# Turning q and k on TensorE instead of by DMA, with three score products over half the partitions

## The chip, the cores and the metric

The kernel runs on one core of a Trainium2 chip. The metric is the device time of one launch in microseconds (us). The engines are named as in the profile: PE is TensorE's matmuls and PEld its weight loads, DVE is VectorE, ACT ScalarE, POOL GpSimd, SP SyncE, which issues every DMA of this kernel from one queue.

## What is computed

Attention with queries that are averaged in pairs, over 4 batches, 8 heads, 1152 keys and a head size of 64, and then two feed-forward layers over the 2304 tokens that come out of it (width 512, inner width 2048). All in float32:

```python
q_pool = q.reshape(B, H, S // 2, 2, D).mean(axis=3)
scores = scale * np.matmul(q_pool, k.transpose(0, 1, 3, 2))
attn = np.exp(scores - np.max(scores, axis=-1, keepdims=True))
attn = attn / (np.sum(attn, axis=-1, keepdims=True) + 1e-09)
x = np.matmul(attn, v)            # heads side by side: 2304 x 512
h = x @ w_in1;  x = (h * np.cos(h)) @ w_out1
h = x @ w_in2;  out = (h / (1.0 + np.exp(-h))) @ w_out2
```

## The kernel before

TensorE gets float16 only. Every float32 operand is scaled by a power of two and split in a high part, rounded to float16, and a low part, the rest in float16; a product of two such operands is taken from three or four products of parts, summed in PSUM.

**Pairs of heads.** The attention goes through 16 pairs, head j and head j + 4 of one batch. `pair_loads` (L317) loads q, k and v of a pair from SP's queue. `pair_prep` (L341) adds neighbouring rows of q on POOL, takes absolute maxima on DVE, makes the common scales of the pair with a small float32 matmul (`mean_scales`, L122, tile `bm`), and then splits. For q, ACT writes the high part twice and DVE the low part, with a copy, into `qn` (L376 to L383), so that a row of 128 values holds high and low part of one head side by side, and a second arrangement low and high. One DMA transpose (L385) turns its 18 blocks of 128 x 128 into `qT`. For k, `kn` is made the same way and a second DMA transpose (L395) of 18 blocks makes `kT`. v needs no turning (`do_v`, L369).

**Tiles.** A pair has nine score tiles: four of 128 queries for each head, and one that holds the last 64 queries of both. `tile_scores` (L406) multiplies over all 128 partitions: qT's first arrangement (high over low) against kT (high over low) gives two products at once, the second arrangement (low over high) the other two. That is two passes over 1152 keys in pieces of 512, 512 and 128 columns, six matmuls. The remainder tile does it for each head on 64 columns of the array, twelve matmuls. The scores stand in `sp`, a PSUM tile with one buffer. DVE reads it (`sc`, L431), ACT takes the exponential (L438) and the high part (L444), POOL the low part (`hl`, L449), a DMA transpose of 18 blocks turns both (`hlT`, L451), and TensorE multiplies by v (`pv`, L462 and L466) four tiles later.

**Around it.** In the first four pairs DVE, ACT and POOL also decode the weights of the first layer. From the second batch on, `share` puts two units of the first layer between two tiles: `g1_unit` (L534) is 12 matmuls into `h`, `g2_unit1` (L594) 12 into `y`. Tiles `h`, `bm` and the other small matmuls share the two buffers of the PSUM pool `ps_h`. What is left of the first layer then runs beside the decoding of the second layer's weights, and the second layer follows. While pair n is worked on, `prep_then_load(n + 1)` prepares the next pair and then loads the one after it.

The order on each engine is made by the tile framework's scheduler when the kernel is built, from priorities (`P_SC`, `P_EX` and so on) and its own estimates; every engine, and SP's queue, then runs its list strictly in that order.

## Time and profile before

| | us |
|---|---|
| median of 3 runs | 1474.19 (1473.89 to 1474.35) |
| the profiled execution | 1469.55 |
| its span, first to last instruction | 1467.3 |

| engine | busy us | share of the span |
|---|---|---|
| PE | 1187.7 | 81% |
| DVE | 990.1 | 67% |
| ACT | 788.3 | 54% |
| POOL | 584.3 | 40% |
| DMA, queue of SP | | 59.5% of 16 engines |

The span has two halves of different kind. In the page's 40 slices the DMA engines are busy for 7 to 9 tenths or more up to slice 24, that is until about 900 us: this is the attention, with the first layer between its tiles. From slice 30 on PE is at 9 tenths or more and the others at 1 to 3: this is the second layer. A share of busy time over the whole span mixes the two, so it is read by stretch.

### The profile page before, as it was taken

The numbers are of one execution on the slowest core, as the hardware profiler recorded it, in microseconds if no ns is written. First come the engines' busy times: TensorE is split into PE (matmuls) and PEld (weight loads), VectorE is DVE, ScalarE is ACT, GpSimd is POOL, SyncE is SP. The second block draws the span as 40 slices with busy tenths as digits, with TensorE's granted clock in tenths as the row PEclk, the third lists the DMA queues.
The fourth block names the chain that finished last, engine by engine and source line by source line (L and its number), as shares of the span: only waits on it lengthen the run. The fifth ranks groups of instructions, "written<-read, shape, count | busy, mean of one in ns | idle before, by whom it ended". The sixth has DMA issues, their size and how long they took to land. (4 is left out here: it accounts for less than half of the span.)

```text
span 1467.3 us, 25115 instructions
## 1 busy us (share of the span) xinstructions
PE 1187.7 (81%) x10070; PEld 867.4 (59%) x10070; DVE 990.1 (67%) x1822; ACT 788.3 (54%) x1005; POOL 584.3 (40%) x329
## 2 busy tenths in 40 slices
PE   1555554787987697788988886788899999999998
PEld 0333332475765465566666765676776666666665
DVE  7999998687775778777888874788963233332312
ACT  3766767568775687767687773645541111111110
POOL 1765664545655466556456452464530000000000
PEclk9875656799998799999999997999999999999999
DMA  8898996978899899869979875324310000000001
GB/s 251 176 229 171 213 233 117 188 146 153 161 179 182 161 189 211 164 127 176 192 146 197 183 133 94 115 87 130 101 46 15 28 29 30 29 30 15 15 1 29
DMA packets 493589, 186.19 MB, mean 127 GB/s; under 512 B 433568, under 2 KB 468384, under 8 KB 493472
## 3 DMA queue, kind: packets, MB, share of 16 engines
q1 hardware_dynamic: 493472, 184.59, 59.5%
q8 instruction: 79, 1.29, 0.4%
q14 instruction: 38, 0.31, 0.1%
HBM read 66.58 MB, written 9.44 MB: 52 GB/s over the span
## 5 line engine op out<-in xcount | busy, mean ns | idle before, releaser
L449 POOL TENSOR_TENSOR hl<-sc,hl 128x1152 f16<-128x1152 f32 x144 | 369.5, 2572 | 250.4 <-ACT hl L444 166.3
L542 PEld LDWEIGHTS <-ih 128*128 128x128 f16 x2304 | 229.9, 101 | 80.3 <-issue 19.3
L555 ACT ACTIVATE hk<-h,ca 128x512 f32<-128x512 f32 x144 | 97.9, 681 | 303.8 <-PE h L542 303.4
L416 PE MATMUL sp<-kT,qT 128*128 128x512 f16 (+1 forms) x768 | 182.2, 383 | 94.6 <-DVE sc L431 83.4
L431 DVE TENSOR_SCALAR_CACHE_REDUCE sc<-sp,psu 128x1152 f32<-128x1152 f32 x144 | 202.9, 1409 | 70.1 <-PE sp L416 55.9
L462 PE MATMUL pv<-vt,hlT 128*128 128x130 f16 (+1 forms) x1440 | 187.3, 243 | 73.5 <-DMA hlT<-hl 61.3
L438 ACT ACTIVATE sc<-sc,nb 128x1152 f32<-128x1152 f32 x144 | 179.8, 1250 | 118.8 <-DVE nb L435 80.7
L462 PEld LDWEIGHTS <-hlT 128*128 128x128 f16 (+1 forms) x1440 | 149.9, 114 | 104.3 <-DMA hlT<-hl 80.1
L542 PE MATMUL h<-xT,ih 128*128 128x256 f16 x1024 | 196.5, 289 | 11.1 <-ACT hk L555 7.1
L542 PE MATMUL h<-ys,ih 128*128 128x256 f16 x1152 | 198.0, 273 | 0.8 <-ACT hk L555 0.8
L466 PE MATMUL pv<-vt,hlT 128*128 128x65 f16 (+1 forms) x1440 | 180.0, 212 | 0.0
L416 PEld LDWEIGHTS <-qT 128*128 128x128 f16 x768 | 76.6, 111 | 168.5 <-issue 131.0
L444 ACT ACTIVATE hl<-sc 128x1152 f16<-128x1152 f32 x144 | 165.3, 1154 | 8.2 <-DMA xT<-xn 3.5
L602 PE MATMUL y<-gh,oh 128*128 128x256 f16 x576 | 159.7, 277 | 6.3 <-ACT y L611 6.3
L602 PE MATMUL y<-gl,oh 128*128 128x256 f16 x576 | 159.6, 277 | 2.6 <-POOL gl L583 2.6
L590 DVE TENSOR_SCALAR gh<-hk,ck 128x1024 f16<-128x1024 f32 x36 | 27.1, 752 | 196.6 <-PE o L623 190.9
L602 PE MATMUL y<-gh,ol 128*128 128x256 f16 x576 | 159.5, 277 | 0.0
L542 PE MATMUL h<-ys,il 128*128 128x256 f16 x576 | 157.1, 273 | 0.0
L466 PEld LDWEIGHTS <-hlT 128*128 128x128 f16 (+1 forms) x1440 | 145.7, 111 | 7.0 <-issue 2.2
L542 PE MATMUL h<-xT,il 128*128 128x256 f16 x512 | 147.9, 289 | 0.0
L542 PEld LDWEIGHTS <-il 128*128 128x128 f16 x1152 | 115.9, 101 | 19.2 <-issue 0.5
L602 PEld LDWEIGHTS <-oh 128*128 128x128 f16 x1152 | 112.7, 99 | 22.7 <-issue 7.5
(291 smaller groups left out, 2093.1 us busy)
## 6 DMA issues: line engine op xcount, KB each, us to landing
wst<-in_moe_w_in_dram SPq DMA_DIRECT2D x32, 512.0 KB, 4.7
wst<-in_moe_w_out_dram SPq DMA_DIRECT2D x32, 512.0 KB, 4.2
stk<-in_k_dram SPq DMA_DIRECT2D x32, 288.0 KB, 3.8
stv<-in_v_dram SPq DMA_DIRECT2D x32, 288.0 KB, 4.1
stq<-in_q_dram SPq DMA_DIRECT2D x32, 256.0 KB, 3.1
ydr<-y SPq DMA_DIRECT2D x9, 512.0 KB, 3.2
y32b<-ydr SPq DMA_DIRECT2D x9, 512.0 KB, 3.7
out_dram<-osb SPq DMA_DIRECT2D x16, 256.0 KB, 3.3
```

The source lines that it names most:

```text
L416: nc.tensor.matmul(sp[:, o:o + n], P.qT[e][:, t, :], kT[:, o:o + n], start=(e == 0), stop=(e == 1))
L431: nc.vector.tensor_scalar(out=T.sc, in0=T.sp, scalar1=T.P.su, scalar2=None, op0=ALU.mult, op1=ALU.max, accum_out=mx)
L438: nc.scalar.activation(out=T.sc, in_=T.sc, func=AF.Exp, bias=nb)
L444: nc.scalar.activation(out=hi, in_=T.sc, func=AF.Copy)
L449: nc.gpsimd.tensor_tensor(out=T.hl[:, 1, :], in0=T.sc, in1=T.hl[:, 0, :], op=ALU.subtract)
L462: nc.tensor.matmul(G.pv[r, T.gi], T.hlT[:, 0, c, r], P.vt[i][:, c], start=(c == 0), stop=(c == KC - 1), skip_group_check=True,)
L466: nc.tensor.matmul(G.pv[r, T.gi, 0], T.hlT[:, 1, c, r], P.vt[i][:, c, 0], start=False, stop=(c == KC - 1), skip_group_check=True,)
L542: nc.tensor.matmul(hp, wt[:, c, f * 128:(f + 1) * 128], xt(c), start=(i == 0), stop=(i == 3 * NC - 1), skip_group_check=True,)
L555: nc.scalar.activation(out=o, in_=blk.hp, func=AF.Copy if first else AF.Silu, scale=blk.c.a[:, g:g + 1])
L590: nc.vector.tensor_scalar(out=gh, in0=hk, scalar1=blk.c.k, scalar2=None, op0=ALU.mult)
L602: nc.tensor.matmul(blk.y[:, oc, :], wt[:, f, oc * 128:(oc + 1) * 128], gt[:, f % 4, :], start=(f == 0 and e == 0 and oc % 2 == 0), stop=(f ...
```

## The change

q and k are no longer split before they are turned. `P.q` holds the two heads of a pair side by side in 128 columns (and zeros in half of the remainder's rows, from two memsets on POOL), `P.k` likewise. `turn` transposes the float32 blocks on TensorE against the identity, up to four blocks into one buffer of `ps_h`: 5 blocks of q and 9 of k for a pair, in chunks of 4, 1, 4, 4 and 1. ACT then scales and rounds the high part out of PSUM and DVE takes the low part, straight into `qT` and `kT`. Both DMA transposes, `qn`, `kn` and the copy are gone. In `qT` and `kT` head j lies in partitions 0 to 63 and head j + 4 in partitions 64 to 127. A score tile is now three products (high x high, high x low, low x high) over the 64 partitions of its head, nine matmuls; the remainder tile is nine matmuls over 128 partitions, with the zeros. Since the heads lie side by side, q is loaded in ten DMAs a pair instead of four, in rows of 256 bytes (before, 2048 bytes and 512 for the remainder), and k in rows of 256 bytes (before, 2304).

```diff
--- before.py
+++ after.py
-NB_N, NB_SC, NB_H, NB_T, NB_S = 2, 4, 4, 4, 5
+NB_SC, NB_H, NB_T, NB_S, NB_K = 4, 4, 4, 3, 1
...
-        P.q = at.src.tile([128, 2 * NT + 1, 2, D], F32, tag="stq", name="stq", bufs=1)
-        P.k, P.v = (
-            [at.src.tile([128, KC, D], F32, tag="stg", name="st" + nm, bufs=NB_S) for i in range(2)] for nm in "kv"
-        )
+        P.q = at.src.tile([128, NT + 1, 2, 2, D], F32, tag="stq", name="stq", bufs=1)
+        P.k = at.src.tile([128, KC, 2, D], F32, tag="stk", name="stk", bufs=NB_K)
+        P.v = [at.src.tile([128, KC, D], F32, tag="stv", name="stv", bufs=NB_S) for i in range(2)]
...
+        for i in range(2):
+            nc.gpsimd.memset(P.q[HALF[i], NT, :, 1 - i, :], 0.0)
         for i, h in enumerate(heads):
-            nc.sync.dma_start(
-                out=P.q[:, i * NT:(i + 1) * NT], in_=q[P.b, h, 0:n, :].rearrange("(p t r) d -> p t r d", t=NT, r=2)
-            )
...
+            for t in range(NT):
+                nc.sync.dma_start(
+                    out=P.q[:, t, :, i, :], in_=q[P.b, h, 0:n, :].rearrange("(p t r) d -> p t r d", t=NT, r=2)[:, t]
+                )
...
+        for i, h in enumerate(heads):
+            nc.sync.dma_start(out=P.k[:, :, i], in_=k[P.b, h].rearrange("(p c) d -> p c d", c=KC))
+            yield
...
-        qn = at.src.tile([128, 2, NQ, 2, D], F16, tag="kn", name="qn", bufs=NB_N)
-        for e in range(2):
-            nc.scalar.activation(out=qn[:, e, :, e, :], in_=qs, func=AF.Copy, scale=s[:, 0:1])
-        nc.vector.scalar_tensor_tensor(
-            out=qn[:, 0, :, 1, :], in0=qs, scalar=s[:, 0:1], in1=qn[:, 0, :, 0, :], op0=ALU.mult, op1=ALU.subtract
-        )
-        nc.vector.tensor_copy(qn[:, 1, :, 0, :], qn[:, 0, :, 1, :])
-        qT = at.p.tile([128, 2, NQ, 128], F16, tag="qT", name="qT", bufs=2)
-        nc.sync.dma_start_transpose(
-            out=qT.rearrange("p e n k -> p (e n) k"), in_=qn.rearrange("p e n s d -> p (e n s d)")
-        )
...
-            split(kn[:, i, :, 0, :], kn[:, i, :, 1, :], P.k[i], s[:, 1:2], P.on_pool >= 1)
...
-        nc.sync.dma_start_transpose(
-            out=kT.rearrange("p i c k -> p (i c) k"), in_=kn.rearrange("p i c s d -> p (i c s d)")
-        )
...
+        P.qT = at.p.tile([128, 2, NT + 1, 128], F16, tag="qT", name="qT", bufs=2)
+        P.kT = at.p.tile([128, 2, KC, 128], F16, tag="kT", name="kT", bufs=2)
+
+        def turn(dst, src, n, col):
+            for o in range(0, n, 4):
+                w = min(4, n - o)
+                tp = ps_h.tile([128, 2, GW], F32, tag="h", name="tp").rearrange("p a b -> p (a b)")[:, 0:w * 128]
+                for c in range(w):
+                    nc.tensor.transpose(tp[:, c * 128:(c + 1) * 128], src(o + c), ident)
+                hi, lo = (dst[:, e, o:o + w, :].rearrange("p c k -> p (c k)") for e in range(2))
+                nc.scalar.activation(out=hi, in_=tp, func=AF.Copy, scale=s[:, col:col + 1])
+                nc.vector.scalar_tensor_tensor(
+                    out=lo, in0=tp, scalar=s[:, col:col + 1], in1=hi, op0=ALU.mult, op1=ALU.subtract
+                )
+                yield
+
+        yield from turn(P.qT, lambda c: qf[:, c, 0, :], NT + 1, 0)
+        yield from turn(P.kT, lambda c: P.k[:, c].rearrange("p h d -> p (h d)"), KC, 1)
...
+    PRODS = ((0, 0), (0, 1), (1, 0))
...
-            for e in range(2):
-                for o, n in segs:
-                    nc.tensor.matmul(sp[:, o:o + n], P.qT[e][:, t, :], kT[:, o:o + n], start=(e == 0), stop=(e == 1))
...
+        r, tt = (HALF[t // NT], t % NT) if t < 2 * NT else (slice(0, 128), NT)
+        for x, (a, c) in enumerate(PRODS):
+            for o, n in segs:
+                nc.tensor.matmul(
+                    sp[:, o:o + n], P.qT[r, a, tt, :], P.kT[r, c, o // 128:(o + n) // 128, :],
+                    start=(x == 0), stop=(x == 2),
+                )
```

The scheduler makes another order of it. On SP the loads of the fourth pair's q (`stq`) surround the two transposes (`hlT` is a tile's own transpose, `stk` and `stv` are loads of k and v, `wst` of weights). Before:

```order
L451 DMA_TRANSPOSE hlT_1167<-hl_1164 128x18x128
L321 DMA stq_1174<-in_q_dram 128x512
L385 DMA_TRANSPOSE qT_965<-qn_960 128x18x128
L395 DMA_TRANSPOSE kT_1076<-kn_999 128x18x128
L324 DMA stq_1174<-in_q_dram 64x128
L321 DMA stq_1174<-in_q_dram 128x512
L324 DMA stq_1174<-in_q_dram 64x128
L330 DMA stk_1176<-in_k_dram 128x576
L451 DMA_TRANSPOSE hlT_1240<-hl_1237 128x18x128
L451 DMA_TRANSPOSE hlT_1305<-hl_1302 128x18x128
L206 DMA wst_1149<-in_moe_w_out_dram 128x8x128
```

After, at the same place:

```order
L325 DMA stq_1279<-in_q_dram 128x2x64
L328 DMA stq_1279<-in_q_dram 64x2x64
L325 DMA stq_1279<-in_q_dram 128x2x64 x3
L439 DMA_TRANSPOSE hlT_1198<-hl_1195 128x18x128
L325 DMA stq_1279<-in_q_dram 128x2x64
L439 DMA_TRANSPOSE hlT_1272<-hl_1269 128x18x128
L328 DMA stq_1279<-in_q_dram 64x2x64
L439 DMA_TRANSPOSE hlT_1355<-hl_1352 128x18x128
L334 DMA stv_1282<-in_v_dram 128x576
L334 DMA stv_1950<-in_v_dram 128x576
L439 DMA_TRANSPOSE hlT_1423<-hl_1420 128x18x128
L331 DMA stk_1280<-in_k_dram 128x9x64 x2
```

The two transposes are gone, the load of q is ten entries, and transposes of score tiles stand between these.

On DVE, in the preparation of the fifth pair (`ps` is the tile of scales, `sc` the reading of a score tile out of PSUM, `nb` its maximum, `den` and `pvs` the end of a group of tiles). Before:

```order
L380 SCALAR_TENSOR_TENSOR qn_2152<-stq_1799,ps__2125,qn_2152 128x9x64
L474 TENSOR_SCALAR den_2324<-pv_2214,ps__1551 128x3
L435 TENSOR_SCALAR nb_2291<-mx_2289 128x1
L480 TENSOR_REDUCE pvs_2327<-pv_2214 128x192
L339 SCALAR_TENSOR_TENSOR kn_2185<-stk_1800,ps__2125,kn_2185 128x9x64
L383 COPY qn_2152<-qn_2152 128x9x64
L478 RECIPROCAL den_2324<-den_2324 128x3
L339 SCALAR_TENSOR_TENSOR kn_2185<-stk_1801,ps__2125,kn_2185 128x9x64
L339 SCALAR_TENSOR_TENSOR vt_2253<-stv_1802,ps__2125,vt_2253 128x9x64
L431 TENSOR_SCALAR sc_2341,mx_2342<-sp_2334,psu_1582 128x1152
L339 SCALAR_TENSOR_TENSOR vt_2276<-stv_1803,ps__2125,vt_2276 128x9x64
```

After, at the same place:

```order
L423 TENSOR_SCALAR nb_2435<-mx_2433 128x1
L368 SCALAR_TENSOR_TENSOR vt_2443<-stv_1950,ps__2277,vt_2443 128x9x64
L466 RECIPROCAL den_2521<-den_2521 128x3
L368 SCALAR_TENSOR_TENSOR vt_2466<-stv_1951,ps__2277,vt_2466 128x9x64
L419 TENSOR_SCALAR sc_2481,mx_2482<-sp_2471,psu_1684 128x1152
L385 SCALAR_TENSOR_TENSOR qT_2304<-tp_2306,ps__2277,qT_2304 128x512
L423 TENSOR_SCALAR nb_2484<-mx_2482 128x1
L385 SCALAR_TENSOR_TENSOR qT_2304<-tp_2334,ps__2277,qT_2304 128x128
L419 TENSOR_SCALAR sc_2544,mx_2545<-sp_2534,psu_1684 128x1152
L423 TENSOR_SCALAR nb_2547<-mx_2545 128x1
L385 SCALAR_TENSOR_TENSOR kT_2305<-tp_2364,ps__2277,kT_2305 128x512
L419 TENSOR_SCALAR sc_2586,mx_2587<-sp_2576,psu_1684 128x1152
```

The low part of v moved ahead of those of q and k, the copy is gone, and the low parts of q and k are read from `tp` in PSUM in pieces that stand among the score tiles.

On PE, where the q of the eighth pair is turned, between matmuls of the first layer (`y`, with the weights `oh` and `ol`). Before, at the matmul for the scales:

```order
L602 LDWEIGHTS ol_86
L602 MATMUL y<-gh,ol_86 128x256
L127 MATMUL bm<-pm_4041,mean 128x3
L542 LDWEIGHTS ih_83
L542 MATMUL h<-xT,ih_83 128x256
```

After, a little behind that matmul:

```order
L590 LDWEIGHTS oh_85
L590 MATMUL y<-gl,oh_85 128x256
L590 LDWEIGHTS ol_86
L590 MATMUL y<-gh,ol_86 128x256
L382 MATMUL tp<-ident,stq 128x128 x4
L590 LDWEIGHTS oh_85
L590 MATMUL y<-gh,oh_85 128x256
```

Four transposes into one buffer of `ps_h` now stand between the matmuls of a unit.

## Rows read from the trace of the kernel before

**Rows 1.** Windows: stretch, length, busy us by engine, PEclk, DMA share, GB/s.

```profile
0.00:300.00 300.00, 159.44 (x1198) 102.70 (x1199) 260.17 (x560) 193.59 (x254) 162.62 (x108) 0.72 0.89 195
300.00:900.00 600.00, 500.13 (x5050) 384.98 (x5048) 465.26 (x770) 435.71 (x521) 332.40 (x177) 0.94 0.87 168
1090.00:1467.30 377.30, 372.16 (x2551) 249.35 (x2548) 110.98 (x168) 57.20 (x78) 0.00 (x0) 1.00 0.07 23
```

**Rows 2.** The page's DMA queues and HBM bytes.

```profile
q1 hardware_dynamic: 493472, 184.59, 59.5%
...
HBM read 66.58 MB, written 9.44 MB: 52 GB/s over the span
```

**Rows 3.** Windows of single pairs of heads, and sum over ten pairs.

```profile
482.30:523.60 41.30, 30.64 (x279) 21.29 (x276) 32.70 (x66) 30.69 (x36) 22.00 (x14) 0.83 0.94 167
...
570.60:632.80 62.20, 50.69 (x485) 37.34 (x485) 45.89 (x69) 41.10 (x48) 36.06 (x19) 0.92 0.87 173
...
686.50:735.50 49.00, 44.62 (x416) 32.86 (x417) 40.40 (x71) 32.91 (x37) 24.48 (x17) 0.93 0.94 178
...
sum 521.00, PE 433.11 PEld 330.40 DVE 410.87 ACT 384.81 POOL 292.91; mean PE 43.31 PEld 33.04 DVE 41.09 ACT 38.48 POOL 29.29
```

**Rows 4.** Groups by line and shape: xcount | busy us, mean ns | idle before, releasers.

```profile
L431 DVE TENSOR_SCALAR_CACHE_REDUCE sc<-sp,psu 128x1152 f32<-128x1152 f32 x144 | 202.9, 1409 | 70.1 <-PE sp L416 55.9 <-PE sp L421 8.1 <-POOL hl L449 3.3
...
L542 PE MATMUL h<-xT,ih 128*128 128x256 f16 x1024 | 196.5, 289 | 11.1 <-ACT hk L555 7.1 <-DMA xT<-xn 3.9
...
L416 PE MATMUL sp<-kT,qT 128*128 128x512 f16 x512 | 172.9, 451 | 94.6 <-DVE sc L431 83.4 <-DMA kT<-kn 10.9
...
L462 PE MATMUL pv<-vt,hlT 128*128 128x130 f16 x1152 | 149.2, 239 | 58.3 <-DMA hlT<-hl 46.1 <-DVE pvs L480 8.2 <-DVE pm L355 1.5
...
L416 PEld LDWEIGHTS <-qT 128*128 128x128 f16 x768 | 76.6, 111 | 168.5 <-issue 131.0 <-DMA qT<-qn 3.5
...
L632 DVE TENSOR_TENSOR osb<-o,cy 128x512 f32<-128x512 f32 x18 | 12.3, 686 | 15.5 <-PE o L623 15.5
```

**Rows 5.** Tile kT: ns min/median/max; who waited for the score matmuls (us, times).

```profile
L395 SPq DMA_TRANSPOSE kT<-kn x16: 2432/2804/4083, 21.3 to 801.0; - x16
...
  DVE sc L431: 64.1, 38
```

**Rows 6.** DMA issues: KB each, median us from issue to landing.

```profile
wst<-in_moe_w_out_dram SPq DMA_DIRECT2D x32, 512.0 KB, 4.2
stk<-in_k_dram SPq DMA_DIRECT2D x32, 288.0 KB, 3.8
...
qT<-qn SPq DMA_TRANSPOSE x16, 5.1
```

**Rows 7.** Windows over the whole span, tiles kn and qn alone: DVE and ACT busy.

```profile
0.00:1467.30 1467.30, 32.05 (x32) 22.82 (x32) 0.91 0.60 127
...
0.00:1467.30 1467.30, 25.42 (x32) 22.88 (x32) 0.91 0.60 127
```

**Rows 8.** Timeline of PE at three places: start us, us, instruction.

```profile
600.13 0.22 PE L462 MATMUL pv<-vt,hlT 128*128 128x130 f16 x1
600.18 1.14 PE L416 MATMUL sp<-kT,qT 128*128 128x512 f16 x6
601.16 0.19 PE L466 MATMUL pv<-vt,hlT 128*128 128x65 f16 x1
...
676.60 0.22 PE L462 MATMUL pv<-vt,hlT 128*64 128x130 f16 x1
676.76 0.88 PE L416 MATMUL sp<-kT,qT 128*128 128x512 f16 x4
...
1064.07 0.27 PE L91 MATMUL mt<-ident,wm 128*1 128x128 f32 x1
1064.18 0.27 PE L602 MATMUL y<-gl,oh 128*128 128x256 f16 x1
```

**Rows 9.** Tile bm: weight loads of 128x128 float32, ns min/median/max.

```profile
L127 PEld LDWEIGHTS bm<-pm,mean x32: 186/190/338, 10.9 to 789.6; 128*128 128x128 f32 x32
```

More of the change, by code (lines that the diff above doesn't have):

```diff
@@ L76, in make_consts @@
         nc.vector.memset(halfpi, math.pi / 2)
-        io = pool.tile([128, 128], I32, name="io", tag="kn", bufs=NB_N)
+        io = pool.tile([128, 128], I32, name="io", tag="io", bufs=1)
         nc.gpsimd.iota(io, pattern=[[1, 128]], base=0, channel_multiplier=-1)
@@ L341, in pair_prep @@
-    def pair_prep(at, P):
-        NQ = 2 * NT + 1
-        qs = P.q[:, :, 0, :]
-        nc.gpsimd.tensor_tensor(out=qs, in0=qs, in1=P.q[:, :, 1, :], op=ALU.add)
-        m = small.tile([128, 5], F32, name="pm", tag="pm")
-        for i in range(2):
-            absmax(m[:, 1 + i:2 + i], P.k[i], AX.XY)
-            yield
+            for t in range(NT):
+                nc.sync.dma_start(
+                    out=P.q[:, t, :, i, :], in_=q[P.b, h, 0:n, :].rearrange("(p t r) d -> p t r d", t=NT, r=2)[:, t]
+                )
@@ new lines, in pair_loads @@
+            nc.sync.dma_start(out=P.q[HALF[i], NT, :, i, :], in_=q[P.b, h, n:, :].rearrange("(p r) d -> p r d", r=2))
+            yield
+        for i, h in enumerate(heads):
+            nc.sync.dma_start(out=P.k[:, :, i], in_=k[P.b, h].rearrange("(p c) d -> p c d", c=KC))
+            yield
+        for i, h in enumerate(heads):
+            nc.sync.dma_start(out=P.v[i], in_=v[P.b, h].rearrange("(p c) d -> p c d", c=KC))
+            yield
+    def pair_prep(at, P):
+        qf = P.q.rearrange("p t r h d -> p t r (h d)")
+        qs = qf[:, :, 0, :]
+        nc.gpsimd.tensor_tensor(out=qs, in0=qs, in1=qf[:, :, 1, :], op=ALU.add)
+        m = small.tile([128, 4], F32, name="pm", tag="pm")
+        absmax(m[:, 1:2], P.k.rearrange("p c h d -> p (c h d)"))
+        yield
@@ L383, in pair_prep @@
-        nc.vector.tensor_copy(qn[:, 1, :, 0, :], qn[:, 0, :, 1, :])
-        qT = at.p.tile([128, 2, NQ, 128], F16, tag="qT", name="qT", bufs=2)
-        nc.sync.dma_start_transpose(
-            out=qT.rearrange("p e n k -> p (e n) k"), in_=qn.rearrange("p e n s d -> p (e n s d)")
-        )
-        P.qT = [qT[:, e] for e in range(2)]
-        yield
-        kn = at.src.tile([128, 2, KC, 2, D], F16, tag="kn", name="kn", bufs=NB_N)
-        for i in range(2):
-            split(kn[:, i, :, 0, :], kn[:, i, :, 1, :], P.k[i], s[:, 1:2], P.on_pool >= 1)
-            yield
@@ L394, in pair_prep @@
-        kT = at.p.tile([128, 2, KC, 128], F16, tag="kT", name="kT", bufs=2)
-        nc.sync.dma_start_transpose(
-            out=kT.rearrange("p i c k -> p (i c) k"), in_=kn.rearrange("p i c s d -> p (i c s d)")
-        )
-        P.kT = [kT[:, i].rearrange("p c k -> p (c k)") for i in range(2)]
-        yield
+            nc.scalar.activation(out=vt[:, :, 0, 0:D], in_=P.v[i], func=AF.Copy, scale=s[:, 2:3])
+            nc.vector.scalar_tensor_tensor(
+                out=vt[:, :, 1, 0:D], in0=P.v[i], scalar=s[:, 2:3], in1=vt[:, :, 0, 0:D],
+                op0=ALU.mult, op1=ALU.subtract,
+            )
```

36 lines of the change are left out of this document (7 added, 29 removed).

## The prediction

> **What bounds the kernel now.** I read the windows first (their busy times stand in the order PE, PEld, DVE, ACT, POOL), since busy shares over the whole span mix two programs. From 1090 us on, PE is busy 372.2 of 377.3 us at a granted clock of 1.00, its upper level of 2.4 GHz, with DMA at 0.07 [rows 1]: that is the second layer, PE alone sets it, and the change touches nothing in it. What remains of the first layer after the attention is also untouched, and the order built from the changed kernel puts nearly the same number of first-layer units between the tiles. So only the attention, up to about 900 us, can change, and what it gains or loses moves the rest as a block.
>
> There no engine is full. In the first 300 us DVE is busy 260 us and the clock is at 0.72, that is for more than half of the time at the lower level of 1.2 GHz; from 300 to 900 us PE is busy 500 of 600 us. In both stretches the DMA share is highest or next to it, 0.89 and 0.87 [rows 1]. The single pairs tell more. Ten of them last 521.0 us, 52.1 each, and although one takes 41.3 and another 62.2 us, DMA stays between 0.87 and 0.94 in those shown, while the busy share of PE goes from 0.74 (30.64 of 41.30) to 0.91 (44.62 of 49.00) [rows 3]. The quickest pair is one with DMA at 0.94 and PE at 0.74. I take this as a stage in which DMA is the tightest resource and PE the next.
>
> Last the waits, by line. PE waited 83.4 us for DVE to free the score tile, 46.1 us for hlT (the transposed probabilities), and 10.9 and 3.5 us for kT and qT; DVE waited 55.9 and 8.1 us for scores [rows 4]. No wait dominates. A resource that is relieved gives back only part, one that is loaded more costs only part, and the two parts are what I must choose.
>
> **The change, term by term.** The sum is made against the profiled execution, 1469.55 us, of which the span is 1467.3; the median of the runs lies 4.6 us higher, and I add that at the end.
>
> *DMA out.* All DMA takes 59.5% of the span on 16 engines, 873 us [rows 2]. Plain traffic has a price from the last stretch: 23 GB/s at a share of 0.07, 329 GB/s at full share [rows 1]. HBM traffic of 66.58 + 9.44 = 76.0 MB [rows 2] thus takes 231 us, and the other 642 us are transposes: 144 of 18 blocks for tiles, 32 of 18 for q and k, 8 of 16 and 2 of 8 elsewhere, 3312 blocks, 0.194 us each. The 576 blocks that go cost 112 us, 7.0 a pair. On SP each such transpose holds the queue for 2.8 us (median) [rows 5], so about 90 us of SP's time go too, from in front of the hlT transposes queued behind. Six more loads of q a pair come in.
>
> *DMA in.* q and k of a pair, 1.18 MB, take 3.6 us at that rate. They now come in 4608 rows of 256 bytes, as many packets of that size as the 36 blocks of 128 that go. No load in rows of 256 bytes is in the trace, so I bound it. One end: it costs by its bytes, 0 more. That is supported by the weight loads in rows of 512 bytes, 4.2 us to landing for 512 KB against 3.8 us for 288 KB of k in long rows [rows 6]. Other end: a packet costs what a packet of a transpose costs, 7.0 us a pair, 3.4 more, 54 us in all. Between the ends I take 27. So DMA is relieved by 85 us (58 to 112). I let half of it reach the end, since DMA is tightest but not full: **-42** (0 to -112).
>
> *Waits for qT and kT.* They end: **-14**, the 10.9 and 3.5 us above [rows 4]. What is late next there is the last evacuation of kT, which I count below.
>
> *DVE and ACT.* DVE spends 32.1 us on kn and 25.4 on qn [rows 7]. After, it reads PSUM: 48 pieces of 512 columns at 686 ns, and 32 of 128 for which I estimate 0.25 us from 1409 ns for 1152 columns and 686 for 512 [rows 4]: 41 us. That is 16 us less. Maxima and ACT's work keep their sizes within 2 us. DVE is at 87% early and 78% later [rows 1]; half: **-8** (0 to -18).
>
> *Scores.* Columns through the array a pair: before 8 x 2304 + 4608 = 23040, after 9 x 3456 = 31104. Six matmuls of 2304 columns start at 600.18 and the next one at 601.16 [rows 8], 0.425 ns a column, so 8064 columns more are 3.4 us a pair, 55 us. About five pairs run before 300 us; if all their scores ran at the lower clock it is 17 us more: 72.
>
> *Transposes.* 14 a pair, 224 in all. A float32 transpose of 128 columns is followed by the next matmul after 0.11 us [rows 8]; if the weight load of 128 x 128 float32, 0.19 us [rows 9], is not hidden behind the one before, it is 0.30. That is 25 to 67 us. I take 0.15, near the lower end, since the trace's other weight loads run while a matmul runs: 34.
>
> *Half of the rows.* Between a matmul on 64 columns and the scores on 128, 0.16 us pass (676.60 to 676.76) where without such a switch it is 0.05 (600.13 to 600.18) [rows 8]. I take the same 0.11 us for entering and for leaving scores on 64 partitions: 2 x 128 tiles, 28 us (0 to 28). The Trainium skill, "TensorEngine Tiling (Array Packing)", section "Key Properties", has a rule that speaks against the change here: changing the tiling mode drains TensorE. The trace agrees as far as its 0.11 us can show; with no drain the sum below would be 7 us lower.
>
> Together PE gets 72 + 34 + 28 = 134 us. What reaches the end? DVE waited for scores in 38 of 144 tiles [rows 5], and there PE was what was missing: 26% of 134, **+35** (0 to +134).
>
> *Buffers of ps_h.* 80 chunks take turns with h, each held until ACT and then DVE have read it. PE waited 7.1 us for such an evacuation before 1024 of the h matmuls [rows 4]; with half as many tiles again in the pool I take **+4** (0 to +40, half a microsecond a chunk). Behind a waiting transpose all PE work is queued, and POOL's memset for the next q waits in the same way in front of POOL's low parts.
>
> Sum: -42 - 14 - 8 + 35 + 4 = -25. 1469.55 - 25 = 1444.5, on the median's scale **1449 us**.
>
> **Rivals.**
> *PE becomes the bound (slower).* Ten pairs hold 43.3 us of PE work in 52.1 [rows 3]. Scores 3.4, transposes 2.1 and switches 1.8 make 50.6. The best any shown pair did is 0.91; at that share a pair takes 55.6 us, 3.5 more, and eleven pairs 39. With 10 us won in the first five it is +29: 1503. It decides as soon as PE cannot be packed above 0.97 in 52.1 us. Against it: part of the busy time is half-clock matmuls (clock 0.94 [rows 1]), which a busier PE may lose.
> *The loads eat the relief.* If rows of 256 bytes cost 7 us a pair more, the -42 is gone: +17, 1491. The Trainium skill, "DMA: Bandwidth & Descriptors", section "Specifications", wants 512 bytes or more for the full rate. No load here shows it.
> *DMA is the whole bound.* Then all 85 us count: -85 - 14 - 8 + 35 = -72, 1402. For it: the quickest pair runs at 0.94 DMA; against it: the slow pair, 62.2 us, has DMA at only 0.87 [rows 3].
> *Nothing visible.* Each relief is met by a cost of its size: 1474.
>
> **How the numbers follow.** Forecast 0.38, DMA the whole bound 0.14, nothing visible 0.10, PE the bound 0.28, loads eat the relief 0.10. Faster by over 0.2% (3 us, about what a measurement of this kernel can tell from no change) is 0.38 + 0.14 = 0.52, within it 0.10, slower 0.38. The range: the low end cuts through the DMA rival, 1412, the high end lies just past the PE rival, 1505; the likeliest case's own range is 1430 to 1468.
>
> **What would show it.** Right: attention ends some 25 us sooner, DMA in 300 to 900 us falls to about 0.8, PE's waits for hlT shrink, PE's busy time there rises by 60 us or more, PE from there to the end unchanged. Wrong: pairs longer than 53 us with PE above 0.92 in them; a DMA share that stays near 0.87 with q and k loads that land late; PE idle before the transposes for buffers; DVE waiting for scores far more than 64 us.

## The result, and the profile after

The changed kernel took 1496.71 us (median; 1488.0 to 1502.03) beside 1474.27 us for the kernel before on the same chip: a ratio of 1.0144 with a 95% interval of 1.0095 to 1.0194, 22 us slower. The prediction was 25 us faster, to 1449 us. The profiled execution is the quickest of the changed kernel's, 1488.0 us with a span of 1486.2, 18.9 us longer than the span before. It lies 8.7 us below the median of its kernel, so stretches read from it show less than the 22 us.

Windows of the kernel after, columns as in [rows 1]:

```profile
0.00:300.00 300.00, 207.26 (x1314) 124.48 (x1315) 254.09 (x547) 187.57 (x253) 161.43 (x120) 0.69 0.81 174
300.00:900.00 600.00, 557.87 (x5294) 404.23 (x5294) 442.10 (x766) 433.30 (x530) 319.97 (x193) 0.96 0.75 144
1100.00:1486.20 386.20, 380.99 (x2632) 257.26 (x2629) 113.00 (x170) 59.44 (x83) 0.86 (x1) 1.00 0.08 25
```

Beside [rows 1] the DMA share fell from 0.89 and 0.87 to 0.81 and 0.75, as forecast. PE's busy time rose by 48 and 58 us. DVE's fell by 6 and 23. The last stretch is PE alone again. The page has the same in its DMA line, 52.8% of 16 engines' span, 785 us, where [rows 2] give 59.5% of 1467.3, 873 us: 88 us relieved, forecast 85.

```profile
q1 hardware_dynamic: 483744, 165.72, 52.8%
```

Groups of the kernel after by line and shape (xcount | busy us, mean ns | idle before, releasers), which answer to [rows 4]:

```profile
L409 PE MATMUL sp<-kT,qT 64*128 64x512 f16 x768 | 242.0, 431 | 50.6 <-DVE sc L419 46.7 <-ACT kT L384 1.7 <-DVE pbw L98 1.5
L419 DVE TENSOR_SCALAR_CACHE_REDUCE sc<-sp,psu 128x1152 f32<-128x1152 f32 x144 | 203.0, 1410 | 83.2 <-PE sp L409 78.4 <-PE pv L454 2.8 <-POOL hl L437 1.1
L450 PE MATMUL pv<-vt,hlT 128*128 128x130 f16 x1152 | 152.6, 240 | 37.2 <-DMA hlT<-hl 29.1 <-DVE pvs L468 7.7 <-DVE den L466 0.3
```

PE waits less for DVE (46.7 us beside 83.4) and for hlT (29.1 beside 46.1) than in [rows 4]. DVE waits more for PE, 78.4 us where it was 55.9 and 8.1. These shifts do not tell where 22 us went. The starts of the pairs do. DVE reads the first score tile at 30.5 us before and 31.3 us after, the first tile of the sixth pair at 323.8 and 338.6, the last tile at 886.0 and 903.4. With the stretches cut at these times, the windows of before, then of after (same columns):

```profile
30.50:323.80 293.30, 175.08 (x1376) 117.38 (x1376) 259.21 (x536) 199.13 (x257) 167.85 (x99) 0.71 0.87 184
323.80:886.00 562.20, 470.60 (x4737) 359.81 (x4735) 438.32 (x725) 415.31 (x495) 317.27 (x170) 0.94 0.88 170
```

```profile
31.30:338.60 307.30, 235.70 (x1629) 148.76 (x1629) 260.39 (x547) 204.32 (x270) 173.14 (x112) 0.69 0.77 160
338.60:903.40 564.80, 524.52 (x4984) 378.19 (x4982) 417.09 (x722) 410.64 (x502) 305.58 (x184) 0.96 0.76 146
```

The first five pairs got 14.0 us longer, the other eleven 2.6, what lies before and behind them 2.3. In the eleven, PE went from 84% busy (470.6 of 562.2) to 93%.

**Where the first five pairs lose.** From the first tile of a pair to the first tile of the next, in us:

| pair | 1 | 2 | 3 | 4 | 5 |
|---|---|---|---|---|---|
| before | 49.9 | 67.6 | 62.7 | 48.0 | 65.0 |
| after | 60.1 | 64.8 | 67.2 | 50.6 | 64.7 |

Ten of the 14 us are lost in the first pair, 4.5 in the third. Windows of the first pair, before and then after:

```profile
30.50:80.40 49.90, 28.14 (x153) 16.07 (x153) 47.67 (x107) 36.80 (x46) 33.72 (x16) 0.78 0.83 189
31.30:91.40 60.10, 44.10 (x248) 25.08 (x248) 53.70 (x110) 37.04 (x47) 33.10 (x20) 0.74 0.76 164
```

DVE is busy 6 us longer there and idle 4 us longer (6.4 us beside 2.2, of which 3.6 wait for scores and 2.6 for ACT's `wt`). Most of the longer busy time is decoding of weights: in the new order 29 of its instructions (lines 236 to 247, 28.1 us) stand in this pair, where 22 (22.8 us) stood. The first tile of the second pair shows it. Its last scores end at 84.8 us, and DVE reads it at 91.4, behind other work of its queue:

```profile
83.91 0.91 PE L409 MATMUL sp<-kT,qT 64*128 64x128 f16 x4 [0.33 <-DVE nb L423]
```

```profile
83.53 0.33 DVE L385 SCALAR_TENSOR_TENSOR kT<-tp,ps__348,kT 128x128 f16<-128x128 f32 x1
...
87.19 2.45 DVE L239 TENSOR_SCALAR wt<-wt 128x512 int32<-128x512 int32 x1
...
91.36 1.40 DVE L419 TENSOR_SCALAR_CACHE_REDUCE sc<-sp,psu 128x1152 f32<-128x1152 f32 x1
```

The decoding done early is not won back where less of it is left: in the fourth pair DVE is busy 5.4 us less than before, and waits 12.3 us for scores.

The other suspect is the turning of k, in rows of the tile kT between 31 and 339 us after (ns min/median/max, then first and last start), ACT's three evacuations for pairs 2 to 6 in that order:

```profile
L384 ACT ACTIVATE kT<-tp,ps__348 x3: 342/669/688, 57.4 to 79.3; 128x512 f16<-128x512 f32 x2, 128x128 f16<-128x128 f32 x1
L384 ACT ACTIVATE kT<-tp,ps__980 x3: 353/667/685, 137.9 to 153.6; 128x512 f16<-128x512 f32 x2, 128x128 f16<-128x128 f32 x1
L384 ACT ACTIVATE kT<-tp,ps__1649 x3: 373/685/688, 213.7 to 219.2; 128x512 f16<-128x512 f32 x2, 128x128 f16<-128x128 f32 x1
L384 ACT ACTIVATE kT<-tp,ps__2277 x3: 367/687/687, 265.1 to 272.1; 128x512 f16<-128x512 f32 x2, 128x128 f16<-128x128 f32 x1
L384 ACT ACTIVATE kT<-tp,ps__2822 x3: 345/678/688, 309.4 to 329.2; 128x512 f16<-128x512 f32 x2, 128x128 f16<-128x128 f32 x1
```

Three pieces, two of 0.7 us and one of 0.35 on ACT and on DVE, are spread over 22, 16, 6, 7 and 20 us. That looks worse than it is. Before, k was split on ACT and DVE and then turned by one DMA, and this chain was long as well. From ACT's first piece until kT was complete, in us:

| kT for pair | 2 | 3 | 4 | 5 | 6 |
|---|---|---|---|---|---|
| before | 17.0 | 15.9 | 9.7 | 17.3 | 12.8 |
| after | 26.5 | 16.4 | 6.7 | 7.8 | 20.7 |

The chain is longer for pairs 2 and 6, and there kT is complete 7.5 and 8.5 us before DVE reads the first tile. At pairs 3, 4 and 5 kT is the last thing that the first tile waits for: DVE ends its last piece at 154.3, 220.4 and 272.9 us and reads the first tile at 156.1, 223.3 and 273.9. The start of pair 3 shows what stands between the pieces. Timeline of the kernel after, first PE, then ACT (start us, us, instruction, idle before it and its releaser):

```profile
136.53 1.12 PE L382 MATMUL tp<-ident,stk 128*128 128x128 f32 x4
137.44 0.42 PE L91 MATMUL mt<-ident,wm 128*1 128x128 f32 x1
...
149.01 0.58 PE L113 MATMUL bc<-pbw,ones 1*128 1x1 f32 x2 [3.26 <-DVE pbw L107]
149.52 1.12 PE L382 MATMUL tp<-ident,stk 128*128 128x128 f32 x4
```

```profile
150.38 1.40 ACT L267 ACTIVATE ih<-wst,si 128x512 f16<-128x512 f32 x2 [1.81 <-DVE si L117]
151.69 0.67 ACT L384 ACTIVATE kT<-tp,ps__980 128x512 f16<-128x512 f32 x1
```

Four transposes start at 136.53. Behind them in PE's queue stand mt and bc, the two steps of a weight's scale, which use the same two buffers of ps_h. bc waits for DVE, whose queue holds the weights' decoding, until 149.01, and the next four transposes stand behind bc. ACT's second piece then stands behind ih, which waits for the scale as well. But nothing was lost up to here beyond the first pair: the second pair, which ends at this place, lasts 64.8 us, and 67.6 before, where kT came as one DMA and PE waited 5.12 us for it:

```profile
142.85 2.08 PE L416 MATMUL sp<-kT,qT 128*128 128x512 f16 x6 [5.12 <-DMA kT<-kn]
```

### The profile page after: what moved, and what is told of

Its sections match the earlier page's. It is cut to its first block, busy times and chain, and to the rows that moved or that the text cites. A ratio compares the mean times of both kernels' runs of the same rounds, so it can differ in the third digit from the quotient of the medians.

```text
span 1486.2 us, 26359 instructions
## 1 busy us (share of the span) xinstructions
PE 1310.8 (88%) x10630; PEld 923.4 (62%) x10630; DVE 971.5 (65%) x1822; ACT 784.6 (53%) x1021; POOL 577.5 (39%) x361
## 3 DMA queue, kind: packets, MB, share of 16 engines
q1 hardware_dynamic: 483744, 165.72, 52.8%
## 5 line engine op out<-in xcount | busy, mean ns | idle before, releaser
L437 POOL TENSOR_TENSOR hl<-sc,hl 128x1152 f16<-128x1152 f32 x144 | 356.6, 2480 | 254.1 <-ACT hl L432 155.9
L409 PE MATMUL sp<-kT,qT 64*128 64x512 f16 (+1 forms) x1296 | 286.0, 370 | 58.3 <-DVE sc L419 53.1
L419 DVE TENSOR_SCALAR_CACHE_REDUCE sc<-sp,psu 128x1152 f32<-128x1152 f32 x144 | 203.0, 1410 | 83.2 <-PE sp L409 78.4
L409 PEld LDWEIGHTS <-qT 64*128 64x128 f16 (+1 forms) x1296 | 116.8, 105 | 190.7 <-issue 119.1
L450 PE MATMUL pv<-vt,hlT 128*128 128x130 f16 (+1 forms) x1440 | 190.6, 241 | 39.0 <-DMA hlT<-hl 30.8
L530 PE MATMUL h<-xT,ih 128*128 128x256 f16 x1024 | 188.0, 282 | 8.2 <-ACT hk L543 6.4
L530 PE MATMUL h<-xT,il 128*128 128x256 f16 x512 | 143.7, 281 | 0.0
L571 POOL TENSOR_TENSOR gl<-tt,gh 128x1024 f16<-128x1024 f32 x36 | 89.0, 2472 | 99.9 <-DVE gh L570 85.9
L530 PEld LDWEIGHTS <-il 128*128 128x128 f16 x1152 | 114.7, 100 | 18.9 <-issue 2.1
```

Of the source, the lines that this page charges most:

```text
L409: nc.tensor.matmul(sp[:, o:o + n], P.qT[r, a, tt, :], P.kT[r, c, o // 128:(o + n) // 128, :], start=(x == 0), stop=(x == 2),)
L419: nc.vector.tensor_scalar(out=T.sc, in0=T.sp, scalar1=T.P.su, scalar2=None, op0=ALU.mult, op1=ALU.max, accum_out=mx)
L437: nc.gpsimd.tensor_tensor(out=T.hl[:, 1, :], in0=T.sc, in1=T.hl[:, 0, :], op=ALU.subtract)
L450: nc.tensor.matmul(G.pv[r, T.gi], T.hlT[:, 0, c, r], P.vt[i][:, c], start=(c == 0), stop=(c == KC - 1), skip_group_check=True,)
L530: nc.tensor.matmul(hp, wt[:, c, f * 128:(f + 1) * 128], xt(c), start=(i == 0), stop=(i == 3 * NC - 1), skip_group_check=True,)
L571: nc.gpsimd.tensor_tensor(out=G.gl, in0=t, in1=gh, op=ALU.subtract)
```

## The experiments

Theory A: the third pass over the score tile lies on PE's path and ate the relief of the queues. Rivals: B, the half rows; C, the turning and its buffers; D, the 256-byte rows of the loads; E, there is no relief. All times are medians, ratios are to the kernel before on the same chip, with their 95% interval.

### Edits that let the scheduler plan anew

`two`, `two_early` and `two_late`: no third product, everywhere, in the first five pairs, or in the last eleven.

```diff
-        for x, (a, c) in enumerate(PRODS):
+        prods = PRODS[:2] if P.b * NP + P.j < 5 else PRODS
+        for x, (a, c) in enumerate(prods):
```

> The changed kernel without its third product (low part of q times high part of k is left out everywhere, so the scores lack that term); TensorE then streams two passes of 1152 columns a tile, as the kernel before did. Theory A, the third pass lies on the path and ate the relief of the DMA queues: the time falls from 1497 us to below 1474 us, some 1450 us, since 144 tiles lose 0.48 us or more each. Rival B, the turning on TensorE and its share of the PSUM buffers cost it: it falls by 10 us at most, to about 1490 us. Rival C, the loads in rows of 256 bytes took the relief away: no change, about 1497 us.

> The third product is left out of the first five of 16 pairs of heads only (45 of 144 tiles), where TensorE runs mostly at the lower clock. Theory A (the first five pairs carry the loss): the time falls by 14 to 25 us, to about 1475 to 1483 us. A second form of A, the loss lies evenly over all tiles: it falls by 5/16 of what leaving it out everywhere gives. Rivals B and C: 0 to 4 us less.

> The third product is left out of the last 11 of 16 pairs only (99 of 144 tiles), where TensorE is granted nearly the full clock. Theory A in its first form, the loss lies in the first five pairs, and in the later ones the third pass and the relief of the queues cancel: the time falls by 15 to 45 us (99 tiles by 0.48 us is 48 us if every one lies on the path), to 1450 to 1480 us. If the later tiles are bound by the queues and VectorE as before the change: within 5 us of 1497 us.

Measured: `two` 1474.39 us, 1.0006 (0.9986 to 1.0027); `two_early` 1517.71, 1.0317 (1.0260 to 1.0374); `two_late` 1485.98, 1.0072 (1.0049 to 1.0094). Without the third pass everywhere the kernel is where it was before the change, less than A wanted. But without it in 45 of 144 tiles the kernel is 21 us *slower* than with it. In that run the first five pairs last 307.7 us, as after, and the other eleven, in which nothing was left out, 582.9 in place of 564.8. No work can explain that. What moved is the order in which the scheduler puts the instructions. In `two` and `two_late` the other eleven pairs last 546.0 and 546.9 us, 18 less than after, so with a plan made for it the third pass is worth something there.

`rows128`: all products over 128 rows, so that both heads are summed into the scores. `tp2`: each transpose twice. `longq`: q in long rows.

```diff
-        r, tt = (HALF[t // NT], t % NT) if t < 2 * NT else (slice(0, 128), NT)
+        r, tt = slice(0, 128), (t % NT if t < 2 * NT else NT)
```

```diff
-                for c in range(w):
+                for c in [x for x in range(w) for _ in range(2)]:
```

```diff
+                out=P.q[:, i, 0:NT], in_=q[P.b, h, 0:n, :].rearrange("(p t r) d -> p t r d", t=NT, r=2)
...
-        nc.gpsimd.tensor_tensor(out=qs, in0=qs, in1=qf[:, :, 1, :], op=ALU.add)
+        qs = at.src.tile([128, NT + 1, 2, D], F32, tag="qs", name="qs", bufs=1)
+        qv = P.q.rearrange("p h t r d -> p r t h d")
+        nc.gpsimd.tensor_tensor(out=qs, in0=qv[:, 0], in1=qv[:, 1], op=ALU.add)
```

> The changed kernel with its three products over all 128 rows for every tile, so that both heads are summed into the scores (another result than the reference's): as many columns through TensorE, but no step between half the rows and all of them. If the steps between the two forms of the array, or half a filled array and its clock, cost the time: it falls by 10 to 28 us (the prediction's 28 us of mode steps), to about 1470 to 1487 us. Theory A, the columns alone cost it: within 5 us of the changed kernel, 1490 to 1502 us.

> The changed kernel with each of its 224 transposes of q and k issued twice (the same result). It prices the turning. If the transposes lie on the path: 224 more by 0.11 to 0.27 us (the weight load and the transposing matmul) add 25 to 60 us, to 1520 to 1555 us. Theory A, they lie in TensorE's idle time between tiles: 0 to 8 us more, up to 1505 us.

> The changed kernel with q loaded in rows of 2 KB, two DMAs a head in place of five, and GpSimd's sum writing the interleaved layout to a tile of its own (the same result). If the rows of 256 bytes or the 96 more DMA issues cost: 5 to 15 us less, 1482 to 1492 us. Theory A: within 5 us of the changed kernel, which itself scatters by 14 us.

Measured: `rows128` 1486.99, 1.0075 (1.0049 to 1.0100); `tp2` 1525.91, 1.0336 (1.0289 to 1.0384); `longq` 1516.16, 1.0277 (1.0225 to 1.0330). The last has fewer and longer transfers (451488 packets beside 483744) and is 19 us slower than the changed kernel, as no theory had it. Its queues are busy for 785 us, as in the changed kernel.

`before_noT`: the kernel before with the transposes of the first pair only, which all scores then read. The waits for qT and kT and the entries in SP's queue go with them. `before_k256` and `before_buf`: the kernel before with k in one tile with one buffer, loaded in rows of 256 bytes, or in long rows.

```diff
-        qT = at.p.tile([128, 2, NQ, 128], F16, tag="qT", name="qT", bufs=2)
-        nc.sync.dma_start_transpose(
+        if not first:
+            qT = at.p.tile([128, 2, NQ, 128], F16, tag="qT", name="qT", bufs=1)
+            nc.sync.dma_start_transpose(
...
+            first['q'] = qT
+        qT = first['q']
```

```diff
+        kk = at.src.tile([128, KC, 2, D], F32, tag="stk", name="stk", bufs=1)
+        P.k = [kk[:, :, i, :] for i in range(2)]
+        P.v = [at.src.tile([128, KC, D], F32, tag="stg", name="stv", bufs=3) for i in range(2)]
```

(`before_buf` has the tile as 128 x 2 x KC x D and P.k as its `kk[:, i]`.)

> The kernel before with the DMA transposes of q and k left out for all pairs but the first; all scores are made from the first pair's q and k, so the result is another. It gives the relief of the DMA queues by itself, without any new work on TensorE. The prediction's half: 42 us and the waits for qT and kT 14 us, about 1418 to 1432 us. If all of the packet time lay on the path: 85 us, 1390 us. Rival, the queues are not what ends the path, so that no relief shows: 1465 to 1474 us.

> The kernel before with k alone loaded as the changed kernel loads it: both heads interleaved in one tile, in rows of 256 bytes, one buffer for k and three for v. Rival C, rows of 256 bytes take the queues' time: 5 to 17 us more, 1479 to 1491 us. Theory A: the loads are hidden, 1470 to 1478 us; but the one buffer makes a pair's load wait for the turning of the pair before, which could cost some us as well.

> The kernel before with k's two heads in one tile of their own with one buffer and three buffers for v, as in the kernel with 256-byte rows, but loaded in long rows of 2.3 KB: it tells whether the 19 us gained there come from the rows or from the buffers and the order that goes with them. From the buffers: 1450 to 1465 us. From the rows: 1470 to 1480 us. From that one order: anywhere, away from both.

Measured: `before_noT` 1435.97, 0.9739 (0.9689 to 0.9790); `before_k256` 1456.71, 0.9880 (0.9837 to 0.9924); `before_buf` 1487.96, 1.0102 (1.0084 to 1.0119). E falls: there is relief, 38 us here, 14.7 in the first five pairs (278.6 us) and 17.8 in the other eleven (544.4). D finds no support: the rows of 256 bytes do lengthen the transfers, as the rows of k's loads and of the queue show, of `before_buf` first and then of `before_k256` (KB each, median us to landing; packets, MB, share),

```profile
q1 hardware_dynamic: 493472, 184.59, 59.2%
...
stk<-in_k_dram SPq DMA_DIRECT2D x32, 288.0 KB, 3.7
```

```profile
q1 hardware_dynamic: 526240, 184.59, 61.1%
...
stk<-in_k_dram SPq DMA_DIRECT2D x32, 288.0 KB, 4.4
```

(887 us of 16 engines' time beside 881), but the kernel with them is the faster one, by 31 us. It also beats both the kernel before, by some 18 us, and the changed one, by 40. Whether the layout or its order does that is open; the two runs differ in both.

### The order alone

One number of the plan is changed, the same in both kernels, and no instruction.

```diff
-P_CH, P_SC, P_EX, P_PV, P_MS, P_MU, P_W, P_PR, P_X = 0, 60, 0, -100, 200, 0, 0, 0, 0
+P_CH, P_SC, P_EX, P_PV, P_MS, P_MU, P_W, P_PR, P_X = 0, 60, 0, -99, 200, 0, 0, 0, 0
```

```diff
-LD_PACE = (2, 2)
+LD_PACE = (3, 3)
```

> The kernel before with one number of its plan changed (the priority of the attention products from -100 to -99): the same instructions, another order. It measures what an order is worth without any change of work. If orders scatter the time: it differs from before by 5 us or more either way. If only work decides: within 2 us of before.

> The changed kernel with the same one number of the plan changed: the same instructions, another order. If the changed kernel drew a poor order: it falls by 8 to 20 us, to 1477 to 1489 us. If work alone made it slow: 1492 to 1502 us.

> The kernel before with the loads of q, k and v paced by 3 in place of 2 steps: the same instructions, a third order. If orders scatter the time: it differs from before by 5 us or more either way. If only work decides: within 2 us.

> The changed kernel with the same pace of 3: the same instructions, a third order. If its order was poor: 1475 to 1489 us. If work alone made it slow: 1492 to 1502 us. With the other three, the distance between the two kernels' means over their orders is the work's own part of the 22 us.

| order | before, us | ratio | after, us | ratio |
|---|---|---|---|---|
| its own | 1474.27 | 1 | 1496.71 | 1.0144 (1.0095 to 1.0194) |
| priority -99 | 1477.44 | 1.0021 (0.9995 to 1.0047) | 1503.34 | 1.0211 (1.0180 to 1.0243) |
| pace 3 | 1467.69 | 0.9966 (0.9941 to 0.9990) | 1507.22 | 1.0249 (1.0209 to 1.0290) |

Of these three the changed kernel's own order is, if anything, the best. Over the three, the means of the ratios are 0.9996 and 1.0201, about 2% or 30 us apart, and the edits move a kernel by 3 to 11 us, though only the pace of 3 moves it clear of the intervals. Windows of before and after with the priority -99, then of both with the pace of 3:

```profile
31.30:323.70 292.40, 171.00 (x1378) 114.29 (x1377) 259.82 (x536) 198.87 (x257) 164.47 (x98) 0.73 0.88 184
323.70:885.30 561.60, 467.67 (x4736) 358.86 (x4733) 439.99 (x725) 415.04 (x495) 318.85 (x169) 0.93 0.89 170
```

```profile
31.90:340.30 308.40, 231.88 (x1629) 147.14 (x1629) 258.69 (x547) 204.12 (x270) 174.18 (x112) 0.71 0.78 160
340.30:919.40 579.10, 534.51 (x4957) 380.56 (x4956) 414.62 (x722) 409.73 (x502) 305.44 (x183) 0.94 0.73 143
```

```profile
31.00:329.80 298.80, 178.34 (x1393) 119.01 (x1393) 264.19 (x536) 195.93 (x255) 168.11 (x99) 0.70 0.85 179
329.80:881.10 551.30, 459.41 (x4648) 351.00 (x4648) 444.04 (x722) 410.85 (x493) 314.86 (x166) 0.94 0.91 174
```

```profile
31.40:339.10 307.70, 235.85 (x1629) 149.06 (x1629) 259.19 (x547) 204.20 (x270) 172.61 (x112) 0.70 0.78 160
339.10:911.80 572.70, 526.45 (x5005) 379.40 (x5004) 422.33 (x724) 411.48 (x502) 308.62 (x183) 0.96 0.76 144
```

The first five pairs last 293, 292 and 299 us before and 307, 308 and 308 after: 13 us more in the mean. The other eleven last 562, 562 and 551 before and 565, 579 and 573 after, 14 more in the mean.

These are not three orders everywhere. In the traces of the changed kernel no instruction of the first five pairs changes its place on any engine with either edit, and in the kernel before the priority moves 7 of 619 instructions of DVE in the other eleven pairs and none of DVE's in the first five. So the 13 us come from one order of the changed kernel's first five pairs, run three times; they do not tell its work from its order. And the 2.6 us of the kernel as it was given are partly luck of the execution, which was 8.7 us quicker than the median; how much of it was its order is not known.

### The order held

Here the scheduler sets the order for the kernel as it is, and the instructions are edited afterwards, where they stand. `fix_two` cuts the last product of each tile to one column, `fix_rows128` widens the products to 128 rows, `fix_both` does both, `fix_tp2` puts a second copy ahead of each transpose, and `fix_noT` cuts the DMA transposes of q and k in the kernel before to one block of 18 from the third pair on, with all scores read from the first two pairs' qT and kT. Its transposes stay in SP's queue, and what waits for them still does. The first of them:

```diff
+    for blk in nc.main_func.blocks:
+        out = []
+        for x in list(blk.instructions):
...
+            if op == "InstMatmult" and name.startswith("sp_") and x.stop_tensor_calc:
+                x = copy.replace(x, ins=(size(x.ins[0], (x.ins[0].ap[0], (1, 1))), x.ins[1]), outs=(size(x.outs[0], (x.outs[0].ap[0], (1, 1))),))
+            out.append(x)
+        blk.instructions = out
     r = _run(nc, [arrays], core_ids=[0])
```

The others replace the line with the condition: `fix_rows128` sets the partition count of the operands of line 409 to 128 (both heads are summed, as in `rows128`), `fix_noT` sets `(size(i, (i.ap[0], (1, 128))),)` and `(size(o, (o.ap[0], (128, 1), (1, 128))),)` on the transposes.

> The changed kernel in its own order: after the scheduler has set every engine's order, the last of the three products of each score tile is cut to one column (so nearly all of that product is left out). The runs so far gave between 1474 and 1518 us for edits that let the scheduler plan anew, even 21 us more where work was left out, so the order is now held. If the third pass lies on the path: 144 tiles lose 0.48 us at full clock and more at the lower one, up to 70 to 95 us; by the prediction's share (26% of its 72 us) 19 us, to about 1478 us. If the plan made around it hides it: within 5 us of 1497 us.

> The changed kernel in its own order, every product of the scores widened from 64 to 128 rows after the order was set (both heads summed, another result). With a new order this gave 10 us less. If the half rows cost (steps between the two forms of the array, or the clock granted to a half-filled array): 5 to 28 us less, 1469 to 1492 us. If that was the order: within 5 us of 1497 us.

> The changed kernel in its own order with both cuts made after the order was set: the products widened to 128 rows and the last of three cut to one column (another result). Alone the cuts gave 8 and 6.5 us less. If TensorE's part of the loss is more than each shows alone: 20 us or more less, below 1477 us. If they add: 1482 us. If both remove the same wait: 1487 to 1490 us.

> The changed kernel in its own order, each transpose of q and k issued twice in a row after the order was set (the same result). With a new order the doubling cost 29 us. If that was the transposes themselves: 25 to 35 us more, 1522 to 1532 us. If it was the new order: 0 to 12 us more (the prediction's 26% of 34 us is 9 us), 1497 to 1509 us.

> The kernel before in its own order, the DMA transposes of q and k cut after the order was set to one block of 18 from the third pair on, the scores reading the first two pairs' qT and kT (another result). It prices the relief of the queues without a new order; with a new order it was 39 us. If the relief is real: 30 to 60 us less than before, 1415 to 1445 us, the prediction's value being 56 us. If those 39 us came from the order: 0 to 15 us less, 1460 to 1475 us.

| kernel | us | ratio | against the same order, us |
|---|---|---|---|
| `fix_two` | 1488.83 | 1.0094 (1.0063 to 1.0125) | -8 |
| `fix_rows128` | 1490.17 | 1.0102 (1.0071 to 1.0132) | -7 |
| `fix_both` | 1480.88 | 1.0050 (1.0031 to 1.0069) | -16 |
| `fix_tp2` | 1504.82 | 1.0198 (1.0167 to 1.0230) | +8 |
| `fix_noT` | 1456.99 | 0.9883 (0.9840 to 0.9926) | -17 |

The last column is the distance to 1496.71, for `fix_noT` to 1474.27. The changed kernel's own interval is 0.5% wide on either side, 7 us, so the three single ones are at the edge of what can be told; `fix_both` and `fix_noT` are clear of it. The two parts of the scores add, 8 and 7 to 16. The stretches of `fix_both` and of `fix_noT`:

```profile
31.60:334.40 302.80, 192.56 (x1637) 137.95 (x1637) 263.05 (x547) 204.23 (x270) 171.38 (x112) 0.75 0.79 163
334.40:895.20 560.80, 475.73 (x4991) 372.20 (x4989) 421.09 (x723) 410.23 (x502) 307.25 (x184) 0.95 0.76 147
```

```profile
31.10:324.30 293.20, 175.54 (x1392) 118.28 (x1392) 263.34 (x536) 198.81 (x257) 165.25 (x99) 0.71 0.77 168
324.30:874.30 550.00, 464.06 (x4719) 356.76 (x4718) 442.97 (x724) 414.62 (x495) 314.94 (x168) 0.94 0.78 153
```

`fix_both` takes 43 us of PE's busy time out of the first five pairs (235.70 to 192.56), more than two thirds of what the change put in, and they still last 302.8 us, 9.5 more than before. So theory A alone does not hold there. What is left need not be C: `rows128` and `fix_rows128` are the same instructions in two orders (about half of DVE's instructions in the first five pairs stand elsewhere), and the first five pairs last 299.1 us in one and 308.4 in the other. The window of the first pair of `rows128`, and the pairs one by one:

```profile
31.30:81.70 50.40, 29.61 (x232) 17.16 (x232) 48.99 (x105) 35.50 (x45) 31.55 (x20) 0.85 0.77 163
```

| pair | 1 | 2 | 3 | 4 | 5 |
|---|---|---|---|---|---|
| `rows128` | 50.4 | 64.5 | 71.7 | 48.7 | 63.8 |
| `fix_rows128` | 59.2 | 64.7 | 68.1 | 45.1 | 71.4 |
| `fix_both` | 59.2 | 64.3 | 66.7 | 43.1 | 69.6 |

In the order of `rows128` the first pair holds 25 instructions of the decoding in place of 29, DVE is busy 49 us in place of 54, and the pair's loss is gone, although the three pieces of kT for the second pair start over 19.5 us there too. The other such runs differ both ways: in the first five pairs `two` lasts 311.5 us and `fix_two` 305.4, `tp2` 308.9 and `fix_tp2` 313.7. The order alone thus moves these five pairs by 5 to 9 us. The scores show in the fourth pair, where `fix_both` takes 7.5 us off; the fifth gives 4.9 of them back.

`fix_noT` leaves the first five pairs where they were (293.2 us), though the DMA share there fell from 0.87 to 0.77, and gives 12.2 us in the other eleven; in this execution, the slowest of its four, what lies behind them lasts 6 us longer. Its rows, to be held against [rows 4], show what became of the relief:

```profile
L416 PE MATMUL sp<-kT,qT 128*128 128x512 f16 x512 | 170.8, 446 | 101.7 <-DVE sc L431 98.7 <-DMA kT<-kn 2.6
L462 PE MATMUL pv<-vt,hlT 128*128 128x130 f16 x1152 | 149.3, 239 | 47.3 <-DMA hlT<-hl 38.5 <-DVE pvs L480 6.4 <-DVE pm L355 1.5
```

PE's waits for hlT and kT fell by 7.6 and 8.3 us in these groups, and its wait for DVE to free the score tile rose by 15.3; the span of this execution is 5.2 us shorter than before. Most of what PE no longer waited for the transposes it waited for DVE.

## Why the prediction was wrong

*The relief of the queues (85 us, half of it counted, and 14 us of waits).* The size was right, 88 us. The share that reaches the end was not, and this is the step that failed first: 56 us were counted, and the transposes cut in the kernel's own order give 17. With their entries on SP and the waits for them gone too, and a new order, they give 38. So 17 us are what the queues' time alone is worth in that order; how much of the rest is entries and waits, and how much order, is not known. The prediction took DMA for the tightest resource because its share was highest and the quickest pair had 0.94 [rows 3]. In `fix_noT` the share falls by a tenth in the first five pairs and their time stays, with DVE busy 263 of 293 us; over the whole run PE's waits pass from the transposes to DVE. And `before_k256` keeps its queues busier than the kernel before and is faster. A high share says that transfers are under way, not that somebody waits for them.

*The order, for which the sum has no term.* This is the second failed step. The prediction noted that the new order puts nearly the same number of first-layer units between the tiles, and left it there. Ten of the first five pairs' 14 us lie in the first pair, where the order holds seven more instructions of the decoding on DVE. With the instructions of `fix_rows128` that pair lasts 59.2 us in this order and 50.4 in the order of `rows128`, where it lasted 49.9 before.

*Buffers of ps_h (+4, up to 40).* The waits that were foreseen are there. Of PE's idle time before the transposes some 11 us end with an evacuation of tp or h, most of them in this group:

```profile
L382 PE MATMUL tp<-ident,stk 128*128 128x128 f32 x144 | 31.0, 337 | 9.7 <-DVE qT L385 8.5 <-DVE kT L385 0.8 <-DVE uo L120 0.3
```

What of it reaches the end was not tried: no run shortens the turning. It did not hold up the end of the first pair, where the scores of the next tile were ready 6.5 us before DVE read them; a part of the third pair's 4.5 us is possible.

*PE's extra work (134 us, 26% counted, +35).* Between the first and the last tile PE's busy time rose by 114.5 us (645.68 to 760.22); the 28 us of steps between half and whole rows that the prediction assumed would not show as busy. Scores over more columns: 80 us busy forecast as 72, worth 8 us with the order held, and 22 (`two`) with a new one; forecast 19. Half rows: 7 us, at the edge of what can be told, forecast 7. The transposes' rows, between first and last tile of the kernel after (PE, PEld, DVE, ACT),

```profile
31.30:338.60 307.30, 17.59 (x70) 11.61 (x70) 14.16 (x25) 13.36 (x25) 0.69 0.77 160
338.60:903.40 564.80, 27.11 (x140) 17.00 (x140) 28.38 (x50) 26.39 (x50) 0.96 0.76 146
```

are 44.7 us for 210, 0.21 us each where 0.15 was taken, within the bounds; a second set costs 8 us, forecast 9. Together that is about 23 us with the order held. The share of a quarter held up in this order, a little too high; a new order gave other values for each.

*DVE and ACT (-8).* DVE's busy time between the first and last tile fell by 20 us (697.53 to 677.48), forecast 16. What that was worth was not tried.

*Loads in rows of 256 bytes.* 27 us of the queues' time were taken for q and k; k alone cost 6 us of it between `before_buf` and `before_k256`, about half of what was taken for it, and the kernel that had it was the faster one. Long rows for q (`longq`) took nothing off the 785 us.

With the values measured in the held order the sum reads -17 for the queues and +23 for PE, +6, beside +22 measured. The other 16 us stay open. The order of the decoding and the waits of the turning are the candidates that the traces show; no run prices either in the changed kernel as it is, so the cause of these 16 us is not shown. With new orders the three terms were -38, +22 and +29 us, so a sum over two orders would prove little.

Of the rivals, "PE becomes the bound" gave 1503 us and lies nearest, but not for its reason. It let the first five pairs win 10 us, and they lost 14; it put the other eleven at 55.6 us each, and they last 51.3 (52.0 over the three runs), with PE 93% busy, below its 0.97. "The loads eat the relief" is refuted by the 88 us. The signs named for the forecast came in part: the DMA share and the waits for hlT moved as said, PE's busy time nearly (58 us of the 60 or more), while the attention ended 17 us later. Such signs show that the work moved as planned; they say nothing of what it is worth.

## What to carry to other kernels

Where a scheduler makes the order, an edit changes the work and the order at once. Editing the instructions after the order is set prices the work in a plan made for other work; a new plan prices both together. Here the third product came to 8 us one way and 22 the other, so a price belongs to the order it was taken in. Before runs count as several orders, compare the orders in the stretch that is read: here three runs repeated one. Follow a lost stretch down to its parts before a chain is blamed that looks stretched, and hold the chain against the one it replaced. And when a resource is relieved, look at which wait grows: here PE waited 16 us less for the transposes and 15 us more for DVE.
